# A spectral filter whose column table is stored as even columns, then odd ones, with the weight products on DVE shifted by one channel

## The chip, the cores and the metric

The kernel runs on one core of one Trainium2 chip. The metric is the time of one execution in microseconds (us), as the device counts it; smaller is better. The five engines run their own queues in order and meet through semaphores: TensorE (PE; its weight loads are listed apart as PEld), VectorE (DVE), ScalarE (ACT), GpSimd (POOL) and SyncE (SP), which issues most of the DMA transfers.

## The reference

The input `x` has 2048 rows and 576 columns in bfloat16. The first half is a layer norm, a two-dimensional real FFT, a product with a complex weight per frequency, the inverse FFT, and the addition of `x`. The second half is a layer norm and a gated feed-forward network with 4608 hidden columns, added to its own input.

```python
def _A_ref(x, w_r, w_i):
    B, S, D = x.shape
    X = rfft2(x.astype(jnp.float32), axes=(-2, -1))
    W = w_r + 1j * w_i
    X = X * W
    y = irfft2(X, s=(S, D), axes=(-2, -1)).astype(jnp.bfloat16)
    return y

def _B_ref(x, w_gate, w_up, w_down):
    return (_gelu(x @ w_gate) * (x @ w_up)) @ w_down

h = x + _A_ref(_layernorm(x), w_r, w_i)
h2 = h + _B_ref(_layernorm(h), w_gate, w_up, w_down)
```

## The kernel before

All transforms are matrix products with tables of sines and cosines that the kernel builds itself. The work goes through four stages.

1. **Norm and first row step.** `x` is loaded, normalised row block by row block on DVE, and multiplied on PE by a small table (`row16`, lines 248 to 273). ACT writes the outcome to `Bt`. Beside that, DVE, POOL and ACT build the tables: `DT` and `D3` (columns, lines 307 to 309), from which POOL later fills `DF` (lines 360 and 361) and DVE fills `DI` (line 394, in `late_tables`).
2. **The channel loop** (lines 576 to 602). Eight channels go through it in the order 1, 2, ..., 7, 0. For each channel, `f2` multiplies a part of `Bt` by the column table (12 matmuls of 290 columns, line 439), separately for even and odd output columns, and ACT writes the two halves interleaved into `pq`. `f3` combines them with twiddle factors (8 matmuls of 289 columns, lines 454 and 455), and ACT writes `g` and `hs`. DVE then forms sum and difference (`xab`, lines 481 and 482), two products with the weights (`m`, line 499, twice the size), `za` and `zb` (lines 505 and 506) and two outputs `Zt` (lines 508 and 509): eight DVE instructions for a channel, each pair reading what the pair before wrote. `i3` is the first inverse step: 12 matmuls of 256 columns (lines 533 and 534) with parts of `Zt` as weights, whose results ACT writes to `EO`.
3. **Inverse columns and the addition to `h`.** `inv_cols` (line 559) multiplies `EO` by the column table, ACT scales the outcome into `cs`, `add_rows` (line 635) forms output rows, the second half of them by reading `cs` backwards, and `add_h` (line 646) adds them to `h_sb`. Then follow the second norm's statistics, `norm2` and `flip`, a transposing DMA that puts the normalised rows into `Bt` as `hl`. The groups from the sixth on are added during stage 4.
4. **The feed-forward network** (lines 728 to 780): four row blocks, each with 36 blocks of gate and up products (line 741) and then the down products (line 761).

The order of the instructions on each engine is the order in which the program writes them (`manual_schedule`). In round `i` of the channel loop PE gets, one behind the other: `f2` of channel i, the first half of `f3` of channel i-1, the first third of `i3` of channel i-3, the second half of `f3`, the second third of `i3`, the rest of `f2`, the last third of `i3`. DVE gets all eight instructions of channel i-1 in round i. So the first `i3` of a channel stands on PE two rounds behind the DVE work that it needs. Tiles in PSUM have four buffers, `Zts` has three, `xab`, `g` and `hs` two each.

The lines that say this:

```python
        if 1 <= i <= n:
            f3(order[i - 1], 0)
        if i >= 3 and not last:
            i3(order[i - 3], 0)
        if 1 <= i <= n:
            f3(order[i - 1], 1)
            wmul(order[i - 1], i)
```

Of the kernel before, what the change touches and what calls it, by code (L numbers as in the profile page):

```python
# [9 lines left out]
ACT = mybir.ActivationFunctionType  # L10
# [14 lines left out]
DH = D // 2  # L25
J = D // 2 + 1
JP = J + 1
F = 4608
NFT = F // P
NR = D // 64  # L30
# [9 lines left out]
def kernel_body(  # L40
# [62 lines left out]
    G16 = keep.tile([P, 2, 2, P], BF16, name="G16")  # L103


    DT = keep.tile([P, 2, 2, JP], BF16, name="DT")
    DF = keep.tile([P, 2, JP], BF16, name="DF")
    DI = keep.tile([P, 2, J], BF16, name="DI")
    mv = keep.tile([P, H, 2], FP32, name="mv")
    rstd = keep.tile([P, H], FP32, name="rstd")  # L110
    mv2 = keep.tile([P, H, 2], FP32, name="mv2")
# [72 lines left out]
    iD = tmp("iD", [P, 3], FP32)  # L184
    iota(iD[:], [[P, 3]], 0, 1)
    iJ = tmp("iJ", [P, JP], FP32)
    iota(iJ[:], [[1, JP]])
    make_identity(nc, ident[:])
    rev = tmp("rev", [P, 1])
    iota(rev[:], [[0, 1]], 2 * P - 1, -2)  # L190
# [107 lines left out]
            normalise(V, xn[:, h, :], mv, rstd, h)  # L298
            row16(h)

    D3 = tmp("D3", [P, 2, JP], BF16)
    pr, ab = tmp("pr", [P, 9, P]), tmp("ab", [P, 9, P], FP32)
    wm = [tmp(n, [P, 8 * J], BF16) for n in ("wm_r", "wm_i")]
    xn_pool = tc.tile_pool(name="xn", bufs=1, side="right")
    xn = xn_pool.__enter__().tile([P, H, D], BF16, name="xn")

    def col_sin(r, src, bias):
        A.activation(DT[:, 0:2, r, :], src[:, 0:2], ACT.Sin, bias=bias[:], scale=-2.0 * PI / D)
        A.activation(D3[:, r, :], src[:, 2], ACT.Sin, bias=bias[:], scale=-2.0 * PI / D)

    for h in range(1, 12, 2):
        ln_act(h)
# [44 lines left out]
    evict4(4)  # L357
    evict(8)
    norms(12, 14)
    G.tensor_copy(DF[0:32, :, :], D3[0:32, :, :])  # L360
    G.tensor_copy(DF[96:128, :, :], D3[96:128, :, :])
    evict(10)
    evict4(8)
    norms(14, 16)
# [26 lines left out]
            V.tensor_scalar(w[:, :, 0 : J : J - 1], w[:, :, 0 : J : J - 1], 0.5, None, op0=ALU.mult)  # L391

    def late_tables():
        V.tensor_copy(DI[0 : J - 2 * P, :, :], D3[0 : J - 2 * P, :, 0:J])
        pt = two("pt")
        for x in range(2):
            for p0 in (0, 64):
                T.matmul(
                    pt[p0 : p0 + 64, 0, x * P : (x + 1) * P],
                    lhsT=F16[:, 0, 64 * x : 64 * x + 64],  # L400
                    rhs=ident[:],
                    start=True,
                    stop=True,
                )
        for sign in range(2):
            A.activation(
                G16[:, sign, :, :].rearrange("p x q -> p (x q)"),
                pt[:, 0, 0 : 2 * P],
                ACT.Copy,
                scale=G_SCALE if sign == 0 else -G_SCALE,  # L410
            )
# [10 lines left out]
    NS, C, SN = 0, 1, 2  # L422
    pq = {}
    xab = {}
    zt = {}
    order = [1, 2, 3, 4, 5, 6, 7, 0]

# [4 lines left out]
    def f2(c):  # L432
        ps = two("pq_ps")
        if c == 1:
            fill(ps[:, 0, :], 4)
        col = slice(slot[c] * P, (slot[c] + 1) * P)
        for par in range(2):
            for t in (par, par + 2, 4):
                T.matmul(  # L439
                    ps[:, par, 0:JP],  # L440
                    lhsT=Bt[:, t, col],
                    rhs=DT[:, t // 2, :, par:JP:2] if t < 4 else DF[:, :, par:JP:2],
                    start=(t == par),
                    stop=(t == 4),
                )
        sb = wk.tile([P, 2, JP], BF16, name="pq", tag="pq", bufs=6)
        (V.tensor_copy if c == 9 else A.copy)(
            sb[:].rearrange("p r (j a) -> p r j a", a=2),
            ps[:, :, 0:JP].rearrange("p a (r j) -> p r j a", r=2),
        )  # L450
        pq[c] = sb
# [5 lines left out]
    def f3(k, half):  # L457
        ps = two("gh_ps")
        if k == 0:
            p0, p8 = pq[0], pq[8]  # L460
            t0, t1 = (NS, C) if half else (C, SN)
            for b, kk, p in ((0, 0, p0), (1, 8, p8)):
                comb(ps[:, b, 0:J], kk, t0, p[:, 0, 0:J], t1, p[:, 1, 0:J])
            if half == 0:
                xab[k] = wk.tile([P, 2, 2, JP], BF16, name="xab", tag="xab", bufs=2)
            A.copy(xab[k][:, half, :, 0:J], ps[:, :, 0:J])
            return
        p, q = pq[k], pq[k + 8]
        gh = wk.tile([P, 2, JP], BF16, name="hs" if half else "g", tag="hs" if half else "g", bufs=2)
        for r in range(2):  # L470
            if half:
                comb(ps[:, 1 - r, 0:J], k, C, q[:, r, 0:J], NS, p[:, r, 0:J])
            else:
                comb(ps[:, r, 0:J], k, C, p[:, r, 0:J], SN, q[:, r, 0:J])
        A.copy(gh[:, :, 0:J], ps[:, :, 0:J])
        if half == 0:
            xab[k] = gh
            return
        g, hs = xab[k], gh
        x = xab[k] = wk.tile([P, 2, 2, JP], BF16, name="xab", tag="xab", bufs=2)  # L480
        V.tensor_tensor(x[:, 0, :, 0:J], g[:, :, 0:J], hs[:, :, 0:J], ALU.subtract)  # L481
        V.tensor_tensor(x[:, 1, ::-1, 0:J], g[:, :, 0:J], hs[:, :, 0:J], ALU.add)  # L482

    def wmul(k, i):
        x = xab[k]
        z = Zts[i % 3]
        zt[k] = z
        zv = z[:, 0 : 4 * JP].rearrange("p (a b j) -> p a b j", a=2, b=2)
        sl = slice(k, 18 - k, 17 - 2 * k) if k else slice(0, 9, 8)
        m1, m2 = (wk.tile([P, 2, 2, JP], BF16, name=n, tag=n, bufs=1) for n in ("m1", "m2"))  # L490
        if k:
            za, zb = (wk.tile([P, 2, JP], BF16, name=n, tag=n, bufs=1) for n in ("za", "zb"))
        else:
            za, zb = zv[:, 0], zv[:, 1]

        for j0, j1 in ((0, J),) if k else ((0, P), (P, J)):
            js = slice(j0, j1)
            for w, m in ((WR, m1), (WI, m2)):
                V.tensor_tensor(  # L499
                    m[:, :, :, js],  # L500
                    x[:, :, :, js],
                    w[:, sl, js].unsqueeze(1).to_broadcast([P, 2, 2, j1 - j0]),
                    ALU.mult,
                )
            V.tensor_tensor(za[:, :, js], m1[:, 0, :, js], m2[:, 1, :, js], ALU.subtract)  # L505
            V.tensor_tensor(zb[:, :, js], m1[:, 1, :, js], m2[:, 0, :, js], ALU.add)  # L506
            if k:
                V.tensor_tensor(zv[:, 0, :, js], za[:, :, js], zb[:, ::-1, js], ALU.add)  # L508
                V.tensor_tensor(zv[:, 1, :, js], zb[:, ::-1, js], za[:, :, js], ALU.subtract)  # L509
# [44 lines left out]
    def inv_cols(x, g):  # L554

        ps = two("cs_ps")
        for e in range(2):
            for jt in range(NJT):
                T.matmul(  # L559
                    ps[:, e, 0:J],  # L560
                    lhsT=EO[x][:, e, jt, 2 * g : 2 * g + 2].rearrange("p h e k l -> p (h e k l)"),
                    rhs=DT[:, jt, e, 0:J] if jt < 2 else DI[:, e, :],
                    start=(jt == 0),
                    stop=(jt == NJT - 1),
                )
        t = eop.tile([P, 2, JP], BF16, name="cs", tag="cs", bufs=H)
        if x == 0 or g:
            A.activation(t[:, :, 0:J], ps[:, :, 0:J], ACT.Copy, scale=Y_SCALE)
        else:
            A.activation(t[:, 0, 0:J], ps[:, 0, 0:J], ACT.Copy, scale=Y_SCALE)  # L570
            V.tensor_scalar(t[:, 1, 0:J], ps[:, 1, 0:J], Y_SCALE, None, op0=ALU.mult)
        cs[x, g] = t


# [1 line left out]
    for i in range(n + 1):  # L576
        last = i >= n
        if not last:
            f2(order[i])
        if i == 0:  # L580
            twiddles()
# [3 lines that stand above are left out]
            i3(order[i - 3], 0)  # L585
        if 1 <= i <= n:
            f3(order[i - 1], 1)
            wmul(order[i - 1], i)
        if i >= 3 and not last:
            i3(order[i - 3], 1)  # L590
        if not last:
            f2(order[i] + 8)
        if i == 0:
            weights()
        if i >= 3:
            for jt in range(0 if last else 2, NJT):
                i3(order[i - 3], jt)
        if i == 1:
            late_tables()
            scr_pool.__exit__(None, None, None)  # L600
            eop = ctx.enter_context(tc.tile_pool(name="eop", bufs=1, side="right"))
            EO = [eop.tile([P, 2, NJT, H, 2, 4, 8], BF16, name=f"EO{x}") for x in range(2)]
# [23 lines left out]
    def add_rows(g):  # L626


        ys = [two("y_ps") for _ in range(2)]
        for b, sl in ((0, slice(0, DH)), (1, slice(DH, 0, -1))):  # L630
            for x in range(2):
                for t in range(2):
                    for i in range(2):
                        rows = slice(64 * i, 64 * i + 64)
                        T.matmul(  # L635
                            ys[i][:, b, 0:DH],
                            lhsT=G16[rows, b * t, x, :],
                            rhs=cs[x, g][rows, t, sl],
                            start=(x == t == 0),
                            stop=(x == t == 1),  # L640
                        )
        return ys

    def add_h(h, ys):
        hv = h_sb[:, h, :].rearrange("p (b n) -> p b n", b=2)
        V.tensor_tensor(hv, hv, ys[h % 2][:, :, 0:DH], ALU.add)  # L646

    def add_both(g):
        ys = add_rows(g)
# [177 lines left out]
```

## Time and profile before

| What | Value |
|---|---|
| Time, median of 3 runs | 516.52 us (516.24 to 517.73) |
| Time of the profiled execution | 516.51 us |
| Its span from first to last instruction | 514.7 us |
| PE busy | 499.4 us (97%) |
| DVE busy | 207.4 us (40%) |
| ACT busy | 153.5 us (30%) |
| Channel loop, from the first sum on DVE to its last output | 35.5 to 63.8 us |
| First gate product | 85.45 us |

The profile's page shows the engines' shares, the granted clock (0.9 or more in all 40 slices) and the chain of work that ended last. A timeline lists instructions by start, duration, engine, line and tile; what stands in brackets is idle time before the instruction and what ended it. Weight loads (PEld) run beside matmuls, and matmuls overlap each other, so the distance between two starts says more than the duration.

### The profile page before, as it was taken

To read this page: it belongs to the slowest core of one execution; us is meant where nothing else is said; L and a number is where in the kernel's file an instruction comes from. 1 tells how busy PE (TensorE), PEld (TensorE's weight loads), DVE (VectorE), ACT (ScalarE), POOL (GpSimd) and SP (SyncE) were. 2 spreads that over 40 slices of the span, in tenths; PEclk is the share of its full clock that TensorE was granted. 3 is DMA by queue.
4 is the path that set the end of the run, shared out by engine and by line. 5 is a ranking of instruction groups with operands and counts; after the bars stand their busy time and mean duration, and the time that the engine had idled before them with its cause. 6 is when DMAs were issued, how large, how long until landed. Compare 5 with 4: busy or idle time off the path is not lost.

```text
span 514.7 us, 9918 instructions
## 1 busy us (share of the span) xinstructions
PE 499.4 (97%) x4369; PEld 295.3 (57%) x4369; DVE 207.4 (40%) x381; ACT 153.5 (30%) x262; POOL 34.7 (7%) x94
## 2 busy tenths in 40 slices
PE   6989998999999999999999999999999999999996
PEld 2457765555556774444467754444577544444774
DVE  8979957566551103533321034433301133333000
ACT  7789974232221002332310013233200133323000
POOL 8700011111110000000000000000000000000000
PEclk9999999999999999999999999999999999999999
DMA  8964049799773008997840069987600487780000
GB/s 277 256 126 137 1 139 221 145 175 198 140 140 67 1 1 184 196 191 159 159 83 0 1 141 185 209 157 156 122 1 0 107 156 162 155 159 3 13 13 24
DMA packets 88459, 61.25 MB, mean 119 GB/s; under 512 B 24288, under 2 KB 87136, under 8 KB 88416
## 3 DMA queue, kind: packets, MB, share of 16 engines
q1 hardware_dynamic: 88128, 59.44, 56.7%
q0 software_dynamic: 288, 1.18, 0.7%
q8 instruction: 34, 0.56, 0.5%
q14 instruction: 9, 0.07, 0.1%
HBM read 52.65 MB, written 2.36 MB: 107 GB/s over the span
## 4 chain that ended last, share of the span: by engine, by line
PE 87%; DVE 9%; ACT 1%; POOL 1%; DMA 1%; issue 1%; DVEq 0%; POOLq 0%; ACTq 0%
PE gu L741 54%; PE acc L761 28%; DVE m L499 2%; PE f2t L258 2%; PE y_ps L635 1%; PE cs_ps L559 1%; PE f2t L246 1%; DMA Bt<-hrow 1%; DVE za L505 1%; DVE Zt L508 1%; PE f L267 1%; DVE xab L481 1%; DVE zb L506 1%; DVE xab L482 1%; DVE Zt L509 1%
## 5 line engine op out<-in xcount | busy, mean ns | idle before, releaser
L741 PE MATMUL gu<-Bt,wgu 64*128 64x512 bf16 x2592 | 281.0, 376 | 0.7 <-DMA Bt<-hrow 0.7
L741 PEld LDWEIGHTS <-wgu 64*128 64x128 bf16 x2592 | 131.2, 94 | 148.4 <-issue 1.7
L749 ACT ACTIVATE g_sb<-gu 128x512 f32<-128x512 f32 x144 | 86.0, 597 | 306.0 <-PE gu L741 306.0
L750 DVE TENSOR_TENSOR P_sb<-g_sb,gu 128x512 bf16<-128x512 f32 x144 | 98.7, 685 | 162.3 <-ACT g_sb L749 162.3
L761 PEld LDWEIGHTS <-P_sb 128*128 128x128 bf16 x1152 | 112.4, 98 | 30.6 <-issue 2.4
L761 PE MATMUL acc<-wd_b,P_sb 128*128 128x288 bf16 x768 | 99.3, 286 | 0.0
L773 DVE TENSOR_TENSOR h_sb<-h_sb,acc 128x576 bf16<-128x576 bf16 x15 | 11.3, 754 | 119.1 <-PE acc L761 119.1
L761 PE MATMUL acc<-wd_a,P_sb 128*128 128x288 bf16 x384 | 52.3, 286 | 0.5 <-DVE h_sb L769 0.5
L246 PE MATMUL f2t<-h_sb,ident 128*128 128x512 bf16 x41 | 12.4, 425 | 4.4 <-DMA h_sb<-in_A_x_dram 4.4
L660 DVE TENSOR_SCALAR hrow<-h_sb,mv,rstd 128x1152 bf16<-128x1152 bf16 x16 | 13.8, 865 | 1.9 <-POOL rstd L135 1.9
L135 POOL TENSOR_TENSOR rstd<-rstd,mhalf 128x1 f32<-128x1 f32 (+2 forms) x21 | 14.0, 666 | 1.8
L559 PE MATMUL cs_ps<-DT,EO 128*128 128x289 bf16 x64 | 12.4, 287 | 0.6 <-DVE h_sb L646 0.4
L439 PE MATMUL pq_ps<-DT,Bt 128*128 128x290 bf16 x64 | 12.9, 292 | 0.0
L134 POOL TENSOR_SCALAR rstd<-mv 128x1 f32<-128x1 f32 (+2 forms) x21 | 4.8, 229 | 114.1 <-DVE mv L119 113.3
L646 DVE TENSOR_TENSOR h_sb<-h_sb,y_ps 128x576 bf16<-128x576 bf16 x16 | 11.3, 745 | 2.1 <-PE y_ps L635 2.1
L533 PE MATMUL eo_ps<-TI,Zt 128*128 128x256 bf16 x48 | 11.7, 273 | 0.0
L534 PE MATMUL eo_ps<-TI,Zt 128*128 128x256 bf16 x48 | 11.5, 274 | 0.2
L124 ACT ACTIVATE junk<-h_sb 128x576 bf16<-128x576 bf16 x16 | 10.7, 671 | 2.5 <-DMA h_sb<-in_A_x_dram 2.0
L559 PEld LDWEIGHTS <-EO 128*128 128x128 bf16 x96 | 9.0, 97 | 4.3 <-issue 1.3
L246 PEld LDWEIGHTS <-ident 128*128 128x128 bf16 x45 | 4.7, 105 | 11.3 <-issue 4.9
L258 PE MATMUL f2t<-F,xn 128*128 128x256 bf16 x64 | 9.7, 274 | 1.6 <-DVE xn L138 1.6
L439 PEld LDWEIGHTS <-Bt 128*128 128x128 bf16 x96 | 9.2, 97 | 3.0
(113 smaller groups left out, 247.0 us busy)
## 6 DMA issues: line engine op xcount, KB each, us to landing
wgu<-in_B_w_gate_dram SPq DMA_DIRECT2D x48, 432.0 KB, 5.1
wgu<-in_B_w_up_dram SPq DMA_DIRECT2D x48, 432.0 KB, 6.6
wd_b<-in_B_w_down_dram SPq DMA_DIRECT2D x2, 1728.0 KB, 8.3
h_sb<-in_A_x_dram SPq DMA_DIRECT2D x3, 576.0 KB, 7.3
wd_a<-in_B_w_down_dram SPq DMA_DIRECT2D x1, 1728.0 KB, 9.1
out_dram<-h_sb SPq DMA_DIRECT2D x3, 576.0 KB, 3.3
WR<-in_A_w_r_dram SPq DMA_DIRECT2D x1, 650.2 KB, 10.0
WI<-in_A_w_i_dram SPq DMA_DIRECT2D x1, 650.2 KB, 15.9
```

What stands on the lines that cost most here:

```text
L135: G.tensor_tensor(dst[:, sl], dst[:, sl], mhalf[:, sl], ALU.pow)
L246: T.matmul(dst, lhsT=ident[:], rhs=h_sb[:, 2, 0:512], start=True, stop=True)
L258: T.matmul(f2t[:, h % 2, t * 2 * P : (t + 1) * 2 * P], lhsT=x[:, d0 : d0 + P], rhs=F16[:, n : n + 2, :], start=(n == 0), stop=(n == 1),)
L439: T.matmul(ps[:, par, 0:JP], lhsT=Bt[:, t, col], rhs=DT[:, t // 2, :, par:JP:2] if t < 4 else DF[:, :, par:JP:2], start=(t == par), stop=( ...
L533: T.matmul(ps[:, b], lhsT=zl(*z0), rhs=TI[:, kk_, 1:3, :], start=True, stop=False)
L534: T.matmul(ps[:, b], lhsT=zl(*z1), rhs=TI[:, kk_, 0:2, :], start=False, stop=True)
L559: T.matmul(ps[:, e, 0:J], lhsT=EO[x][:, e, jt, 2 * g : 2 * g + 2].rearrange("p h e k l -> p (h e k l)"), rhs=DT[:, jt, e, 0:J] if jt < 2 e ...
L660: V.tensor_scalar(hrow[:], h_sb[:, h, :].rearrange("p (r k) -> p r k", k=64).unsqueeze(2).to_broadcast([P, NR, 2, 64]), mv2[:, h, 0:1], rs ...
L741: T.matmul(gu[:, c, :], lhsT=w[rows, r, i * P : (i + 1) * P], rhs=hl[tcnk % 2][rows, r, :], start=(r == 0), stop=(r == NR - 1),)
L749: A.activation(g_sb[:], gu[:, 0, :], ACT.Gelu_apprx_tanh)
L750: V.tensor_tensor(P_sb[:, fa + i, :], g_sb[:], gu[:, 1, :], ALU.mult)
L761: T.matmul(acc[:, c, 0:DH], lhsT=P_sb[:, f, st * P : (st + 1) * P], rhs=wd_a[:, f, cc] if f < NWA else wd_b[:, f - NWA, cc], start=(f == 0 ...
```

## The change

Two things are changed.

The column tables `DT`, `DF`, `DI` (and `D3`, from which the last two are filled) hold the even columns first and then the odd ones, 145 of each, with the cosine or sine part as an inner index. `f2` reads 290 elements that lie next to each other, where it read every second element. `inv_cols` reads two runs of 145 elements, where it read one run of 289, and makes one more column. Its results `cs` stay in the even-then-odd order. `add_rows` reads `cs` in two runs of 144, and so `y_ps` holds the even columns and then the odd ones; `add_h` puts them back in place by reading and writing `h_sb` with a step of two elements.

In the channel loop, DVE's sums (now `sums_of`) and the rest (`wmul`) are written in other rounds. Round i gives DVE the two products and `za`, `zb` of channel i-2, then the two sums of channel i-1, then the two `Zt` of channel i-2. The first channel's sums stand alone in round 1, and the last channel (0), whose `xab` ACT writes, gets its DVE work at the end of the last round. The order on PE and ACT stays.

```diff
-    DT = keep.tile([P, 2, 2, JP], BF16, name="DT")
-    DF = keep.tile([P, 2, JP], BF16, name="DF")
-    DI = keep.tile([P, 2, J], BF16, name="DI")
+    DT = keep.tile([P, 2, 2, 2, JH], BF16, name="DT")
+    DF = keep.tile([P, 2, 2, JH], BF16, name="DF")
+    DI = keep.tile([P, 2, 2, JH], BF16, name="DI")
...
-    iota(iJ[:], [[1, JP]])
+    iota(iJ[:], [[1, 2], [2, JH]])
...
     def col_sin(r, src, bias):
-        A.activation(DT[:, 0:2, r, :], src[:, 0:2], ACT.Sin, bias=bias[:], scale=-2.0 * PI / D)
-        A.activation(D3[:, r, :], src[:, 2], ACT.Sin, bias=bias[:], scale=-2.0 * PI / D)
+        s = src[:].rearrange("p t (a j) -> p t a j", a=2)
+        A.activation(DT[:, :, :, r, :], s[:, 0:2], ACT.Sin, bias=bias[:], scale=-2.0 * PI / D)
+        A.activation(D3[:, :, r, :], s[:, 2], ACT.Sin, bias=bias[:], scale=-2.0 * PI / D)
...
-        V.tensor_copy(DI[0 : J - 2 * P, :, :], D3[0 : J - 2 * P, :, 0:J])
+        V.tensor_copy(DI[0 : J - 2 * P], D3[0 : J - 2 * P])
...
-                    rhs=DT[:, t // 2, :, par:JP:2] if t < 4 else DF[:, :, par:JP:2],
+                    rhs=DT[:, t // 2, par] if t < 4 else DF[:, par],
...
-        g, hs = xab[k], gh
+        hk[k] = gh
+
+    def sums_of(k):
+        g, hs = gk[k], hk[k]
         x = xab[k] = wk.tile([P, 2, 2, JP], BF16, name="xab", tag="xab", bufs=2)
         V.tensor_tensor(x[:, 0, :, 0:J], g[:, :, 0:J], hs[:, :, 0:J], ALU.subtract)
         V.tensor_tensor(x[:, 1, ::-1, 0:J], g[:, :, 0:J], hs[:, :, 0:J], ALU.add)
 
-    def wmul(k, i):
+    def wmul(k, i, nxt=None):
...
             V.tensor_tensor(zb[:, :, js], m1[:, 1, :, js], m2[:, 0, :, js], ALU.add)
+            if nxt:
+                sums_of(nxt)
             if k:
                 V.tensor_tensor(zv[:, 0, :, js], za[:, :, js], zb[:, ::-1, js], ALU.add)
...
-                    ps[:, e, 0:J],
+                    ps[:, e, 0:JP],
                     lhsT=EO[x][:, e, jt, 2 * g : 2 * g + 2].rearrange("p h e k l -> p (h e k l)"),
-                    rhs=DT[:, jt, e, 0:J] if jt < 2 else DI[:, e, :],
+                    rhs=DT[:, jt, :, e, :] if jt < 2 else DI[:, :, e, :],
...
             f3(order[i - 1], 1)
-            wmul(order[i - 1], i)
+            if i == 1:
+                sums_of(order[0])
+            else:
+                wmul(order[i - 2], i - 1, order[i - 1])
...
+        if last:
+            wmul(order[i - 1], i)
...
-        for b, sl in ((0, slice(0, DH)), (1, slice(DH, 0, -1))):
+        for b in range(2):
             for x in range(2):
+                if b == 0:
+                    cv = cs[x, g][:].rearrange("p t (q a) -> p t q a", q=2)[:, :, :, 0 : JH - 1]
+                else:
+                    cv = cs[x, g][:, :, 1:J].rearrange("p t (q a) -> p t q a", q=2)[:, :, :, ::-1]
...
-                            rhs=cs[x, g][rows, t, sl],
+                            rhs=cv[rows, t],
...
-        hv = h_sb[:, h, :].rearrange("p (b n) -> p b n", b=2)
-        V.tensor_tensor(hv, hv, ys[h % 2][:, :, 0:DH], ALU.add)
+        hv = h_sb[:, h, :].rearrange("p (b a q) -> p b q a", b=2, q=2)
+        V.tensor_tensor(hv, hv, ys[h % 2][:, :, 0:DH].rearrange("p b (q a) -> p b q a", q=2), ALU.add)
```

More of the change, by code (lines that the diff above doesn't have):

```diff
@@ L27 @@
 JP = J + 1
+JH = JP // 2
 F = 4608
@@ L299, in norms @@
             row16(h)
-    D3 = tmp("D3", [P, 2, JP], BF16)
+    D3 = tmp("D3", [P, 2, 2, JH], BF16)
     pr, ab = tmp("pr", [P, 9, P]), tmp("ab", [P, 9, P], FP32)
@@ L359, in kernel_body @@
     norms(12, 14)
-    G.tensor_copy(DF[0:32, :, :], D3[0:32, :, :])
-    G.tensor_copy(DF[96:128, :, :], D3[96:128, :, :])
+    G.tensor_copy(DF[0:32], D3[0:32])
+    G.tensor_copy(DF[96:128], D3[96:128])
     evict(10)
@@ L424, in kernel_body @@
     xab = {}
+    gk, hk = {}, {}
     zt = {}
@@ L476, in f3 @@
         if half == 0:
-            xab[k] = gh
+            gk[k] = gh
             return
-        g, hs = xab[k], gh
+        hk[k] = gh
+    def sums_of(k):
+        g, hs = gk[k], hk[k]
         x = xab[k] = wk.tile([P, 2, 2, JP], BF16, name="xab", tag="xab", bufs=2)
@@ L567, in inv_cols @@
         if x == 0 or g:
-            A.activation(t[:, :, 0:J], ps[:, :, 0:J], ACT.Copy, scale=Y_SCALE)
+            A.activation(t[:], ps[:, :, 0:JP], ACT.Copy, scale=Y_SCALE)
         else:
-            A.activation(t[:, 0, 0:J], ps[:, 0, 0:J], ACT.Copy, scale=Y_SCALE)
-            V.tensor_scalar(t[:, 1, 0:J], ps[:, 1, 0:J], Y_SCALE, None, op0=ALU.mult)
+            A.activation(t[:, 0, :], ps[:, 0, 0:JP], ACT.Copy, scale=Y_SCALE)
+            V.tensor_scalar(t[:, 1, :], ps[:, 1, 0:JP], Y_SCALE, None, op0=ALU.mult)
         cs[x, g] = t
```

## The prediction

> **What bounds the kernel now.** I read the page first, for the chain that ended last, then busy time by stage, the chain in order of time around the end of the channel loop, and the timelines of DVE, PE and ACT inside the loop.
>
> ```profile
> span 514.7 us, 9918 instructions
> ...
> PE 87%; DVE 9%; ACT 1%; POOL 1%; DMA 1%; issue 1%; DVEq 0%; POOLq 0%; ACTq 0%
> ```
>
> PE holds 87% of the chain, nearly all in the feed-forward stage, which the change doesn't touch. DVE's 9% is where the change can act. The next row is the stretch of the channel loop: length, then busy time of PE, PEld, DVE, ACT and POOL.
>
> ```profile
> 29.80:63.90 34.10, 33.17 (x260) 24.29 (x260) 30.36 (x65) 30.87 (x50) 0.00 (x0) 1.00 0.29 80
> ```
>
> Three engines are nearly full here. Whichever is relieved, another stands close behind, so the question is not how much DVE saves but where PE stands then. The chain, in order of time (start, length, what):
>
> ```profile
> 63.39 0.38 DVE Zt L509
> ...
> 63.81 0.28 PE eo_ps L534
> 64.10 0.11 PE eo_ps L533
> ...
> 71.95 1.41 DVE h_sb L646 x2
> ...
> 76.66 0.66 DVE h_sb L646
> ...
> 81.89 3.42 DMA Bt<-hrow
> ...
> 85.45 4.69 PE gu L741 x41
> ```
>
> Up to 63.8 us DVE's last `Zt` sets the end; from there PE, then three additions to `h_sb` with norm work between, the last flip, and the gate products. What is won before 63.8 us is handed down to the end if the later links keep their length.
>
> The DVE timeline: the loop's first sum, the `DI` copy, one full channel, and the loop's last output.
>
> ```profile
> 35.48 0.47 DVE L481 TENSOR_TENSOR xab<-g,hs 128x578 bf16<-128x578 bf16 x1 [0.69 <-ACT hs L475]
> ...
> 39.44 0.30 DVE L394 COPY DI<-D 33x578 bf16<-33x578 bf16 x1
> 39.66 0.45 DVE L481 TENSOR_TENSOR xab<-g,hs 128x578 bf16<-128x578 bf16 x1
> ...
> 51.59 0.46 DVE L481 TENSOR_TENSOR xab<-g,hs 128x578 bf16<-128x578 bf16 x1
> 51.96 0.46 DVE L482 TENSOR_TENSOR xab<-g,hs 128x578 bf16<-128x578 bf16 x1
> 52.45 0.77 DVE L499 TENSOR_TENSOR m<-xab,WR 128x1156 bf16<-128x1156 bf16 x1
> 53.13 0.76 DVE L499 TENSOR_TENSOR m<-xab,WI 128x1156 bf16<-128x1156 bf16 x1
> 53.93 0.47 DVE L505 TENSOR_TENSOR za<-m,m 128x578 bf16<-128x578 bf16 x1
> 54.31 0.46 DVE L506 TENSOR_TENSOR zb<-m,m 128x578 bf16<-128x578 bf16 x1
> 54.87 0.47 DVE L508 TENSOR_TENSOR Zt<-za,zb 128x578 bf16<-128x578 bf16 x1
> 55.25 0.46 DVE L509 TENSOR_TENSOR Zt<-zb,za 128x578 bf16<-128x578 bf16 x1
> 55.62 0.46 DVE L481 TENSOR_TENSOR xab<-g,hs 128x578 bf16<-128x578 bf16 x1
> ...
> 63.30 0.46 DVE L509 TENSOR_TENSOR Zt<-zb,za 128x578 bf16<-128x578 bf16 x1
> ```
>
> DVE never idles: 4.03 us from sum to sum (51.59 to 55.62). An instruction that doesn't read the one right before it starts 0.37 us after a 578-element one, before that one has ended (51.59 to 51.96; 55.25 to 55.62). One that does read it waits for its end: 0.49 (51.96 to 52.45), 0.80 against 0.68 (53.13 to 53.93), 0.56 (54.31 to 54.87).
>
> PE in the same stretch: starts of the first `i3` matmuls of each round, six `f2` matmuls, and the inverse columns behind the loop.
>
> ```profile
> 39.60 0.27 PE L534 MATMUL eo_ps<-TI,Zt 128*128 128x256 bf16 x1
> ...
> 43.75 0.28 PE L534 MATMUL eo_ps<-TI,Zt 128*128 128x256 bf16 x1
> ...
> 47.71 0.28 PE L534 MATMUL eo_ps<-TI,Zt 128*128 128x256 bf16 x1
> ...
> 48.98 0.42 PE L439 MATMUL pq_ps<-DT,Bt 128*128 128x290 bf16 x2
> ...
> 49.76 0.27 PE L533 MATMUL eo_ps<-TI,Zt 128*128 128x256 bf16 x1
> ...
> 51.46 0.27 PE L533 MATMUL eo_ps<-TI,Zt 128*128 128x256 bf16 x1
> 51.74 0.28 PE L534 MATMUL eo_ps<-TI,Zt 128*128 128x256 bf16 x1
> ...
> 55.76 0.28 PE L534 MATMUL eo_ps<-TI,Zt 128*128 128x256 bf16 x1
> ...
> 61.05 0.41 PE L559 MATMUL cs_ps<-DT,EO 128*128 128x289 bf16 x2
> ...
> 62.91 0.41 PE L559 MATMUL cs_ps<-DT,EO 128*128 128x289 bf16 x2
> ...
> 63.16 0.28 PE L559 MATMUL cs_ps<-DI,EO 128*128 128x289 bf16 x1
> ...
> 63.94 0.27 PE L533 MATMUL eo_ps<-TI,Zt 128*128 128x256 bf16 x1
> ```
>
> In each round PE stops at the second `i3` matmul until `Zt` is there. Without that stop a round would take 51.46 + 0.11 - 47.71 = **3.86 us** (0.11 is the regular distance in the chain's rows). The four rounds from 39.60 to 55.76 took 16.16; four times 3.86 is 15.44, so PE lost 0.72 there. At the end, the row of 63.94 would stand at 63.16 + 0.12 + 0.11 + 0.11 = 63.50: 0.44 more. **PE loses 1.16 us** to DVE in all. DVE may save more than that, and it won't show.
>
> **The change part by part, against the profiled execution (516.51 us, 0.01 under the median of the runs, 1.8 over its span).**
>
> *DVE's order.* The eight instructions stay, but three pairs now have others between them. A round's distances become: product to product 0.68, product to `za` 0.80 (still dependent), 0.38, `zb` to sum 0.37, 0.37, sum to `Zt` 0.37, 0.38, `Zt` to next product 0.37: **3.72 us** instead of 4.03. So DVE becomes faster than PE's 3.86.
>
> *Where `Zt` comes later.* The first channel's `Zt` now stands behind the second channel's sums and the `DI` copy. The first sum starts at 35.44 (six faster `f2` matmuls ahead of it, below); then 35.81, the copy at 36.18, products at 36.40 (0.22 behind the copy, as 39.44 to 39.66) and 37.08, `za` 37.88, `zb` 38.26, sums 38.63 and 39.00, `Zt` 39.37 and 39.75, done at 40.21. PE's second `i3` matmul starts 0.05 after that (63.30 + 0.46 to 63.81), at 40.26, where it was 39.60. **A new wait of 0.66 us.** Behind it PE's queue holds the second half of `f3`, and behind that ACT's `hs` and DVE's next sums.
>
> *Does PE wait again?* `Zt` of round n is done at 40.21 + 3.72n, PE arrives at 40.26 + 3.79n: no. The sums need `hs`, and these two rows of ACT give its place:
>
> ```profile
> 52.82 0.65 ACT L475 CAST hs<-gh_ps 128x578 bf16<-128x578 f32 x1 [0.34 <-PE gh_ps L455]
> ...
> 56.85 0.64 ACT L475 CAST hs<-gh_ps 128x578 bf16<-128x578 f32 x1 [0.34 <-PE gh_ps L455]
> ```
>
> `hs` ends 1.73 after the second `i3` matmul (51.74 to 53.47). In the fifth round that is 40.26 + 15.16 + 1.73 = 57.15; DVE comes to those sums at 38.63 + 18.60 = 57.23, so there is just no wait. ACT is busy 4.03 - 0.34 = 3.69 of a round and fits into 3.79. The last `Zt` of channel 7 (dependent again, no sums between) is done near 62.0, and PE gets to it at 63.0: DVE, late by up to a microsecond, would still be covered.
>
> *`f2` read without gaps.* Six matmuls take 49.76 - 48.98 = 0.78, so 0.130 each; inverse columns, read in one run, take (62.91 - 61.05) / 15 = 0.124. The only difference in what PE reads as the moving operand is the step of two. I take 0.124 for `f2` after: 12 x 0.006 = 0.07 a round, 3.79 instead of 3.86, **0.28** over the four rounds PE is the bound. The lower bound is 0; a gain past 0.28 is excluded by 290 columns against 289.
>
> [...]
>
> *Inverse columns in two runs, one more column.* 48 matmuls stand between the loop and the first addition: 8 calls of six. One column is 0.0004 us each (0.124 / 289): 0.02 in all. For two runs there is no row, since every moving operand here is one run; nearest is one run itself (0) and the stepped one (+0.006, 0.29 in all). I take 0, since one break in 290 elements is nearer to none than to 290 steps. A gain is excluded. The same for `add_rows`, 8 pairs before the first addition: 0 to 0.05.
>
> *Addition with a step of two* (groups up to 150 us: count, busy, mean ns, idle before).
>
> ```profile
> L750 DVE TENSOR_TENSOR P_sb<-g_sb,gu 128x512 bf16<-128x512 f32 x31 | 21.0, 679 | 26.8 <-ACT g_sb L749 26.8
> ...
> L646 DVE TENSOR_TENSOR h_sb<-h_sb,y_ps 128x576 bf16<-128x576 bf16 x16 | 11.3, 745 | 2.1 <-PE y_ps L635 2.1
> ...
> L547 DVE CAST EO<-eo_ps 128x512 bf16<-128x512 f32 x1 | 0.7, 691 | 1.2 <-PE eo_ps L534 1.2
> ```
>
> [...] `EO`, written in scattered runs of eight, costs 691 ns, as `P_sb` in one run does at 679. I take 0. The upper end, half the rate, is +0.60 each; three are on the chain (two at 71.95, one at 76.66), the fourth falls into a wait for POOL.
>
> *At nothing:* the tables' `Sin`, copies and `iota` have the same sizes; the last channel's DVE work moves behind `i3` in the text but stays last on DVE, before 63.0. No DMA moves on SP or POOL; the flips and the loads of stage 4 follow the chain.
>
> **Sum:** 1.16 of waits gone, 0.66 of new wait, 0.28 from `f2`, 0.02 for the column: 1.16 - 0.66 + 0.28 - 0.02 = 0.76. 516.51 - 0.76 = 515.75, so **515.7 us**, 0.15% faster, less than the 0.3% (1.55 us) that I count as told from no change.
>
> **Rivals.**
>
> - *`f2` gains nothing* (the 0.006 has another cause): 516.0.
> - *Two runs cost what a step costs* on inverse columns and rows: +0.34, 516.1.
> - *The new DVE order saves no time.* Were every DVE instruction to start only when the one before has ended its flush, DVE would stay at 4.03 and the last `Zt` where it is: 516.5. The 0.37 against 0.49 in the rows speaks against it. [...]
> - *Slower: the stepped addition.* It decides from 0.76 / 3 = 0.25 us more for one addition. At the upper end, 3 x 0.60 = 1.80 on the way to the last flip: 516.51 - 0.76 + 1.80 = 517.55, and about 518 if the following six additions also hold back the PSUM buffers of the first gate product. For it: no row has a step of one element on DVE. [...]
> - *More than 0.3% faster.* All that the loop holds is 1.16 + 0.28 + 0.04, 1.48 us; it would take a gain that no row shows, 514.9 or less.
>
> **How the numbers follow.** Chances: my forecast 0.56 (its own range 515.4 to 516.0), `f2` nothing 0.08, two runs 0.09, no saving on DVE 0.05, slower 0.12, faster than the loop holds 0.10. The forecast and the three rivals beside it all lie within 0.3%: 0.78. The range, 515.0 to 517.0, takes these in, with the beginnings of the outer two.
>
> **What would show it.** On DVE: sums between `zb` and `Zt`, 3.7 to 3.8 us a round, with gaps ahead of the sums. On PE: one wait of about 0.66 at the first `i3`, near 40.26, none in the rounds behind and none before channel 7; `f2` distances of 0.124, inverse columns unchanged. The addition's mean near 745 ns. The first gate product near 84.7. I am wrong if PE still waits for `Zt` in each round, if ACT's `hs` runs late and drags DVE, or if the additions are longer.

## The result, and the profile after

The changed kernel takes 515.74 us in the median of 18 runs (515.4 to 517.11); the kernel before, run beside it, takes 516.48. The ratio is 0.9985, with a 95% interval of 0.9978 to 0.9992: a small gain that is real, 0.74 us in the medians, where 0.76 was forecast. A few runs of either kernel are some 1.3 us longer, and the ratio and its interval count them.

From the page of the changed kernel, the chain that ended last by engine:

```profile
PE 91%; DVE 5%; ACT 1%; POOL 1%; DMA 1%; issue 1%; POOLq 0%; DVEq 0%; ACTq 0%
```

DVE's share of the chain fell from 9% to 5%, PE's rose from 87% to 91%: the loop's bound changed hands. How is seen in the timeline of DVE (start, length, line, tile): the copy of `DI`, the end of the first channel, one full round, and channel 7's last output.

```profile
36.21 0.30 DVE L396 COPY DI<-D 33x580 bf16<-33x580 bf16 x1
...
39.75 0.46 DVE L517 TENSOR_TENSOR Zt<-zb,za 128x578 bf16<-128x578 bf16 x1
...
51.22 0.76 DVE L505 TENSOR_TENSOR m<-xab,WR 128x1156 bf16<-128x1156 bf16 x1
51.89 0.76 DVE L505 TENSOR_TENSOR m<-xab,WI 128x1156 bf16<-128x1156 bf16 x1
52.68 0.47 DVE L511 TENSOR_TENSOR za<-m,m 128x578 bf16<-128x578 bf16 x1
53.06 0.46 DVE L512 TENSOR_TENSOR zb<-m,m 128x578 bf16<-128x578 bf16 x1
53.43 0.46 DVE L487 TENSOR_TENSOR xab<-g,hs 128x578 bf16<-128x578 bf16 x1
53.80 0.46 DVE L488 TENSOR_TENSOR xab<-g,hs 128x578 bf16<-128x578 bf16 x1
54.17 0.46 DVE L516 TENSOR_TENSOR Zt<-za,zb 128x578 bf16<-128x578 bf16 x1
54.54 0.46 DVE L517 TENSOR_TENSOR Zt<-zb,za 128x578 bf16<-128x578 bf16 x1
54.91 0.76 DVE L505 TENSOR_TENSOR m<-xab,WR 128x1156 bf16<-128x1156 bf16 x1
...
61.41 0.46 DVE L517 TENSOR_TENSOR Zt<-zb,za 128x578 bf16<-128x578 bf16 x1
```

A round is 3.69 us (51.22 to 54.91), where it was 4.03. The only distance that still waits for the instruction ahead is the one to `za`, 0.79 (0.67 from product to product). The sum now follows `zb` after 0.37 and `Zt` follows the sum after 0.37.

PE, from the timeline: the first `i3` matmuls, the one wait left behind them, and the third `i3` matmul of channel 7, which stood at 63.94 before.

```profile
39.89 0.28 PE L541 MATMUL eo_ps<-TI,Zt 128*128 128x256 bf16 x1 [0.39 <-DVE Zt L516]
40.26 0.28 PE L542 MATMUL eo_ps<-TI,Zt 128*128 128x256 bf16 x1
...
58.62 0.28 PE L457 MATMUL gh_ps<-pq,TF 128*128 128x289 bf16 x1 [0.38 <-ACT pq L450]
...
63.13 0.27 PE L541 MATMUL eo_ps<-TI,Zt 128*128 128x256 bf16 x1
```

And the chain of waits in order of time, which now runs on PE through the whole loop:

```profile
40.26 0.28 PE eo_ps L542
...
41.69 0.74 PE pq_ps L442 x6
...
71.17 1.47 DVE h_sb L663 x2
...
73.63 0.48 issue
...
81.15 3.38 DMA Bt<-hrow
...
84.67 5.34 PE gu L758 x47
```

Six `f2` matmuls take 0.74 instead of 0.78. The loop hands over 0.81 us earlier (63.94 to 63.13), the first gate product begins 0.78 earlier (85.45 to 84.67), and the span is shorter by about as much (514.7 to 514.0). Below, "the gate" is the start of the first gate product: what is won or lost ahead of it carries over to the end.

### The profile page after: what moved, and what is told of

It is laid out like the page before. It is cut to its first block, busy times and chain, and to the rows that moved or that the text cites. A ratio compares the mean times of both kernels' runs of the same rounds, so it can differ in the third digit from the quotient of the medians.

```text
span 514.0 us, 9918 instructions
## 1 busy us (share of the span) xinstructions
PE 498.3 (97%) x4369; PEld 295.3 (57%) x4369; DVE 206.5 (40%) x381; ACT 153.5 (30%) x262; POOL 34.6 (7%) x94
## 4 chain that ended last, share of the span: by engine, by line
PE 91%; DVE 5%; ACT 1%; POOL 1%; DMA 1%; issue 1%; POOLq 0%; DVEq 0%; ACTq 0%
PE gu L758 55%; PE acc L778 28%; PE f2t L259 2%; PE pq_ps L442 1%; PE cs_ps L567 1%; PE eo_ps L542 1%; PE eo_ps L541 1%; PE y_ps L652 1%; PE f2t L247 1%; DMA Bt<-hrow 1%; PE gh_ps L457 1%; PE gh_ps L458 1%; PE f L268 1%; DVE st L119 0%; DVE h_sb L663 0%
## 5 line engine op out<-in xcount | busy, mean ns | idle before, releaser
L567 PE MATMUL cs_ps<-DT,EO 128*128 128x290 bf16 x64 | 12.5, 286 | 0.6 <-DVE h_sb L663 0.4
L652 PE MATMUL y_ps<-cs,G 64*128 64x288 bf16 x128 | 9.8, 283 | 1.1 <-DVE h_sb L663 0.9
```

The lines of the kernel that those rows point to most:

```text
L567: T.matmul(ps[:, e, 0:JP], lhsT=EO[x][:, e, jt, 2 * g : 2 * g + 2].rearrange("p h e k l -> p (h e k l)"), rhs=DT[:, jt, :, e, :] if jt < 2 ...
L652: T.matmul(ys[i][:, b, 0:DH], lhsT=G16[rows, b * t, x, :], rhs=cv[rows, t], start=(x == t == 0), stop=(x == t == 1),)
```

## Experiments

**The tables alone.** DVE keeps its old order of eight instructions for one channel.

```diff
-            if i == 1:
-                sums_of(order[0])
-            else:
-                wmul(order[i - 2], i - 1, order[i - 1])
+            if order[i - 1]:
+                sums_of(order[i - 1])
+            wmul(order[i - 1], i)
...
-        if last:
-            wmul(order[i - 1], i)
```

> The new column tables with DVE's old order. My theory (DVE's dependent chain sets the end of the loop, so a faster f2 only makes PE wait longer): DVE rounds stay at 4.03 us, first gate product at 85.4 (before: 85.45), time 516.4 to 516.5. Rival (the two parts add up, f2's 0.28 us counts by itself): first gate product near 85.2, time 516.2.

Measured: 516.56 us, ratio to the kernel before 0.9999 (0.9990 to 1.0007). The timelines of DVE and of PE:

```profile
51.58 0.46 DVE L487 TENSOR_TENSOR xab<-g,hs 128x578 bf16<-128x578 bf16 x1
...
55.60 0.46 DVE L487 TENSOR_TENSOR xab<-g,hs 128x578 bf16<-128x578 bf16 x1
```

```profile
85.46 1.90 PE L755 MATMUL gu<-Bt,wgu 64*128 64x512 bf16 x16 [0.62 <-DMA Bt<-hrow]
```

A DVE round is 4.02 us and the gate stays where it was. The faster `f2` is worth nothing while PE waits for DVE anyway.

**DVE's order alone.** The old tables, the stepped reads of `f2`, the addition in one run.

```diff
-    DT = keep.tile([P, 2, 2, 2, JH], BF16, name="DT")
+    DT = keep.tile([P, 2, 2, JP], BF16, name="DT")
...
-                    rhs=DT[:, t // 2, par] if t < 4 else DF[:, par],
+                    rhs=DT[:, t // 2, :, par:JP:2] if t < 4 else DF[:, :, par:JP:2],
```

> DVE's new order with the old column tables and the old addition. My theory: DVE rounds of 3.70 us, PE bound at 3.86 us a round after one wait of 0.7 us; 1.16 - 0.70 = 0.46 us gained, first gate product near 85.0, time 516.05. Rival (DVE's order alone brings all of it and f2 nothing): first gate product at 84.7, time 515.75.

Measured: 515.99 us, ratio 0.9990 (0.9981 to 0.9999). PE's timeline:

```profile
48.02 0.27 PE L541 MATMUL eo_ps<-TI,Zt 128*128 128x256 bf16 x1
...
51.87 0.27 PE L541 MATMUL eo_ps<-TI,Zt 128*128 128x256 bf16 x1
...
84.94 2.33 PE L753 MATMUL gu<-Bt,wgu 64*128 64x512 bf16 x20 [0.71 <-DMA Bt<-hrow]
```

PE's round is 3.85 us without a wait, as computed from the kernel before (3.86), and the gate comes 0.51 us earlier. So the tables alone bring 0.0, DVE's order alone 0.5, both together 0.78: `f2`'s gain counts only once PE is the bound.

**Is the first channel on the path, and the last not?** Two more copies of `DI`'s size in front of the first channel's products, then three in front of channel 7's, each kernel executed once.

```diff
+        if k == 1:
+            for _ in range(2):
+                V.tensor_copy(spare[0 : J - 2 * P], DI[0 : J - 2 * P])
```

> The changed kernel with two more copies of DI's size (0.22 us each, into a spare tile) on DVE ahead of the first channel's products. My theory: all later PE work 0.44 us later, first gate product at 85.1. Rival (DVE's first channel has slack): 84.67.

> The changed kernel with three more copies (0.66 us) ahead of channel 7's products once more, because in the first execution TensorE's clock was at half for a while ahead of the loop and everything stood 1.25 us later. My theory: first gate product at 84.67, as in the changed kernel. Rival (DVE's last Zt still sets the end of the loop): 85.3.

Measured: 516.47 us with the gate at 85.39 for the first, 515.74 us with the gate at 84.68 for the last. Of the run with the copies ahead of the first channel, the copies on DVE and the second `i3` matmul on PE (40.26 in the changed kernel):

```profile
36.55 0.64 DVE L505 COPY spare<-DI 33x580 bf16<-33x580 bf16 x2
```

```profile
40.95 0.28 PE L546 MATMUL eo_ps<-TI,Zt 128*128 128x256 bf16 x1
```

Of the run with the later copies, DVE's timeline and PE's:

```profile
58.64 0.98 DVE L505 COPY spare<-DI 33x580 bf16<-33x580 bf16 x3
...
62.31 0.46 DVE L521 TENSOR_TENSOR Zt<-zb,za 128x578 bf16<-128x578 bf16 x1
```

```profile
62.92 0.27 PE L545 MATMUL eo_ps<-TI,Zt 128*128 128x256 bf16 x1
```

Channel 7's `Zt` is done at 62.77 instead of 61.87 and PE still finds it ready. Ahead of the first channel the two copies cost 0.68 on DVE (each started 0.34 after the copy before it, which it depends on, and not 0.22), PE's first wait grew by 0.69, and the gate moved by 0.72. So DVE's first channel sets the end, one for one, and its last doesn't.

An earlier execution of the second kernel took 517.04 us, with the gate at 85.97: its granted clock was 0.996 in the mean (1.000 in the other), the four matmuls ahead of the first `f2` and the eighteen of `f2` behind them took 1.56 and 3.36 us where the changed kernel's took 1.02 and 2.22, and it stood 1.25 us later from there on (first `f3` matmul at 34.79, 33.54 in the changed kernel). PE found channel 7's `Zt` ready there too (done at 64.01, PE at 64.16). Its expectation:

> The changed kernel with three more such copies (0.66 us) on DVE ahead of channel 7's products. My theory (PE comes to channel 7 about 1.1 us after its Zt): nothing moves, first gate product at 84.67. Rival (DVE's last Zt still sets the end of the loop, as in the kernel before): 85.3.

**More work in front of the first wait.** The first third of `i3` goes behind the second half of `f3` on PE, in every round.

```diff
             f3(order[i - 1], 0)
-        if i >= 3 and not last:
-            i3(order[i - 3], 0)
-        if 1 <= i <= n:
             f3(order[i - 1], 1)
...
         if i >= 3 and not last:
+            i3(order[i - 3], 0)
             i3(order[i - 3], 1)
```

> The changed kernel with the first third of i3 written behind the second half of f3 on PE, so that 0.49 us of matmuls stand ahead of the first wait. My theory: the wait at the first i3 (0.81 us against an unhindered start) shrinks to 0.32, all later PE work moves 0.49 earlier, first gate product at 84.2, time 515.25. Rival (the wait only moves, because ACT or DVE closes the loop at the old place): first gate product between 84.5 and 84.7, time 515.6 or more.

Measured: 515.08 us, ratio 0.9969 (0.9959 to 0.9979), PE's timeline:

```profile
40.27 0.28 PE L542 MATMUL eo_ps<-TI,Zt 128*128 128x256 bf16 x1
...
57.97 0.28 PE L457 MATMUL gh_ps<-pq,TF 128*128 128x289 bf16 x1 [0.22 <-ACT pq L450]
...
84.06 3.20 PE L756 MATMUL gu<-Bt,wgu 64*128 64x512 bf16 x28 [0.66 <-DMA Bt<-hrow]
```

`Zt` comes at the same time, but four more matmuls are done by then. The gate is 0.61 earlier, 0.12 more than the 0.49 of the matmuls. The rest comes from PE's wait for ACT's `pq` in the last round, which is 0.22 here and 0.38 in the changed kernel.

**The `DI` copy on POOL.**

```diff
-        V.tensor_copy(DI[0 : J - 2 * P], D3[0 : J - 2 * P])
+        G.tensor_copy(DI[0 : J - 2 * P], D3[0 : J - 2 * P])
```

> The changed kernel with the copy of DI moved from DVE to POOL. My theory (from the first i3 on PE never stops for DVE, so the first Zt sets everything behind it): the first Zt comes 0.22 us earlier, PE's first wait shrinks by 0.22, first gate product at 84.45 (changed kernel: 84.67), time 515.5. Rival (another engine, ACT's hs or the last DVE work, is the real bound by then): 84.67 and 515.74, unchanged.

Measured: 515.34 us, ratio 0.9984 (0.9973 to 0.9995), the gate at 84.26: 0.41 earlier. But the second `i3` matmul stands at 40.18, only 0.08 earlier. I had counted the copy at its distance of 0.22. In the kernel before, the first product, right behind the sum that it reads, starts 0.49 after it (35.86 to 36.35); in the changed kernel, with the copy between them, 0.59 after it (35.84 to 36.43). The copy mostly stood in that wait, so moving it frees little. The rest arises after the loop, in POOL's timeline, here of the changed kernel and then of this one:

```profile
74.11 0.23 POOL L135 TENSOR_SCALAR rstd<-mv 128x1 f32<-128x1 f32 x1 [47.48 <-DVE mv L120]
```

```profile
73.67 0.23 POOL L135 TENSOR_SCALAR rstd<-mv 128x1 f32<-128x1 f32 x1 [46.31 <-DVE mv L120]
```

In the changed kernel the chain has 0.48 of "issue" ahead of this instruction; here it begins 0.44 earlier though its input came only 0.08 earlier. Counted from its semaphore, POOL begins after 0.50 in the changed kernel (0.02 in its queue and the 0.48) and after 0.13 here (0.02 and 0.11). To tell apart whether that hangs on the copy's being gone from DVE or on one more instruction in POOL's queue, the next kernel leaves the copy on DVE and adds a memset to POOL:

```diff
         V.tensor_copy(DI[0 : J - 2 * P], D3[0 : J - 2 * P])
+        G.memset(DI[96:128], 0.0)
```

> The changed kernel with one more instruction in POOL's queue (a memset of rows of DI that are zero already, right after the table work; the copy of DI stays on DVE). It asks where the 0.41 us of the run with the copy on POOL came from, of which only 0.08 arose in the channel loop; in that run POOL's first instruction after the loop began 0.13 us after its semaphore, against 0.50 in the changed kernel. Theory A (the 0.50 hangs on the instruction's place in POOL's code, so one more instruction anywhere ahead moves it): 0.13 here too, first gate product at 84.3, time 515.4. Theory B (it hangs on the copy being gone from DVE): 0.50, 84.67, 515.74.

Measured: 515.28 us, ratio 0.9971 (0.9962 to 0.9981), with POOL, the chain's row ahead of POOL's, and PE as follows:

```profile
73.76 0.23 POOL L135 TENSOR_SCALAR rstd<-mv 128x1 f32<-128x1 f32 x1 [46.60 <-DVE mv L120]
```

```profile
73.65 0.11 issue
```

```profile
84.36 2.98 PE L759 MATMUL gu<-Bt,wgu 64*128 64x512 bf16 x26 [0.68 <-DMA Bt<-hrow]
```

An added instruction that computes nothing new brings the gate 0.31 us forward (84.67 to 84.36) and the median 0.46. So the copy's being gone from DVE isn't needed, and theory B falls. The length of the wait is no reason either: the kernel with the later `i3` waits 46.84 us on POOL and has 0.49 of issue, this one waits 46.60 and has 0.11. All three kernels with one more instruction on POOL have 0.11, all the others 0.48 or 0.49. But the copy and the memset stand at the same place in POOL's queue, so "anywhere ahead" isn't shown, and the cause of the delay stays open.

**Both together**, the copy on POOL and the later `i3`.

> The changed kernel with the copy of DI on POOL and the first third of i3 behind the second half of f3. My theory: both shorten the same wait, 0.49 and 0.22 of its 0.81 us, so 0.71 together: first gate product at 83.95, time 515.05, faster than both kernels. Rival (only one of the two counts): 84.2, time 515.25.

Measured: 514.64 us, ratio 0.9963 (0.9950 to 0.9975), the gate at 83.59: faster than both kernels. It beats its forecast by 0.4. POOL's earlier start (0.37) was in no term of it; the other two misses, 0.12 too little for the later `i3` and 0.14 too much for the copy, nearly cancel.

**What a step costs PE.** `f2` reads its moving operand from `Bt` in sixteen shapes; the product with the column table is left out (one execution).

```diff
+    reads = [Bf[:, 0:N2], Bf[:, 0:N2], Bf[:, 1 : N2 + 1]]
+    reads += [Bf[:, 0 : 2 * N2 : 2], Bf[:, 1 : 2 * N2 : 2]]
+    reads += [Bf[:, 0 : s * N2 : s] for s in (3, 4, 8, 16, 32)]
...
     def f2(c):
+        rhs = reads.pop(0)
...
-                    rhs=DT[:, t // 2, par] if t < 4 else DF[:, par],
+                    rhs=rhs,
```

> The changed kernel with f2's moving operand taken from Bt in sixteen shapes, one for each call of f2 (the product with the column table is left out, so the output is not the reference's): step 1 (from an even and an odd element), 2 (even, odd), 3, 4, 8, 16, 32; two runs of 145, 29 runs of 10, 145 runs of 2; backwards with step 1 and 2. My theory: distances of 0.124 us for one run, 0.130 for step 2 from either start, 0.124 for two runs, and more than 0.130 for the larger steps. [...]

In PE's timeline a row of six matmuls is six distances long and 0.16 to 0.18 for the tail of the last. In order: step 2 from an even and an odd element; step 3 alone, then 3 and 4; 8; 16; 32; two runs of 145; 29 runs of 10; 145 runs of 2; backwards by 1 and by 2; step 1.

```profile
36.09 0.94 PE L453 MATMUL pq_ps<-Bt 128*128 128x290 bf16 x6
37.20 0.95 PE L453 MATMUL pq_ps<-Bt 128*128 128x290 bf16 x6
38.97 1.33 PE L453 MATMUL pq_ps<-Bt 128*128 128x290 bf16 x6
...
38.97 2.88 PE L453 MATMUL pq_ps<-Bt 128*128 128x290 bf16 x12
43.55 3.23 PE L453 MATMUL pq_ps<-Bt 128*128 128x290 bf16 x6
47.23 3.31 PE L453 MATMUL pq_ps<-Bt 128*128 128x290 bf16 x6
53.83 3.08 PE L453 MATMUL pq_ps<-Bt 128*128 128x290 bf16 x6
57.28 1.66 PE L453 MATMUL pq_ps<-Bt 128*128 128x290 bf16 x6
61.46 0.91 PE L453 MATMUL pq_ps<-Bt 128*128 128x290 bf16 x6
62.64 1.71 PE L453 MATMUL pq_ps<-Bt 128*128 128x290 bf16 x6
66.04 0.91 PE L453 MATMUL pq_ps<-Bt 128*128 128x290 bf16 x6
67.23 0.95 PE L453 MATMUL pq_ps<-Bt 128*128 128x290 bf16 x6
69.87 0.90 PE L453 MATMUL pq_ps<-Bt 128*128 128x290 bf16 x6
```

The clock was not whole throughout: the table of stretches (after each window: its length, the busy time of PE, its weight load, DVE, ACT and POOL, then the granted clock, the DMA share and GB/s) shows two of them at half, 0.50:

```profile
47.20:51.00 3.80, 3.80 (x11) 1.21 (x9) 0.63 (x2) 1.20 (x3) 0.00 (x0) 0.50 0.00 0
...
57.30:60.00 2.70, 2.70 (x13) 1.71 (x12) 0.59 (x2) 1.47 (x4) 0.00 (x0) 0.50 0.00 0
```

| Read | Row, us | One matmul, us |
|---|---|---|
| step 1 | 0.90 | 0.123 |
| step 1 backwards; 29 runs of 10 | 0.91 | 0.125 |
| step 2, even or odd start, backwards | 0.94, 0.95, 0.95 | 0.130 to 0.132 |
| step 3 | 1.33 | 0.195 |
| step 4 | 2.88 less six of 0.195 | 0.258 |
| 145 runs of 2, one in 8 elements | 1.71 | 0.258 |
| step 8 | 3.23 | 0.51 |
| step 16 (half clock), 32 | 3.31, 3.08 | 0.52, 0.48 |
| two runs of 145 (half clock) | 1.66 | 0.25 |

Both of my statements hold: the 0.006 of `f2` comes from the step, whichever element it starts from, and two runs are free: 29 runs of 10 take 0.125 at whole clock, and the two runs of 145 met half clock, where `f3`'s matmuls of 289 columns in one run stand 0.24 apart as well (58.97 to 59.21). Step 4 takes 0.258, twice the 0.123 of step 1.

## Why the prediction was right

- **What bounds.** That DVE's saving counts only up to what PE waits for it is borne out: DVE's last `Zt` came 1.9 us earlier (63.30 to 61.41), but PE's work behind it only 0.81. The two parts of the sum were also measured one by one: 1.16 - 0.66 = 0.50 was forecast for DVE's order, and alone it brought the gate 0.51 forward; 0.26 was forecast for the tables, and they brought 0.27 more.
- **DVE's order.** 3.72 us a round was forecast, 3.69 came. One sign named for DVE, gaps ahead of the sums, didn't show: the sum follows `zb` after 0.37, and after 0.38 in the last round (56.76 to 57.14). That agrees with the prediction's own working, by which `hs` comes just in time (57.15 against 57.23; it ended at 57.10).
- **The new wait.** Forecast: second `i3` matmul at 40.26, 0.66 later than before. It stands at 40.26. That this wait is on the path is shown by the copies ahead of the first channel and by the later `i3`.
- **No wait after it.** PE's rounds run without a stop up to the wait for ACT's `pq` in the last round. The prediction named no such wait and put it at nothing without a reason. The kernel before has it too, and it grew by only 0.04, so the sum holds:

```profile
59.00 0.28 PE L454 MATMUL gh_ps<-pq,TF 128*128 128x289 bf16 x1 [0.34 <-ACT pq L447]
```

  Channel 7's `Zt` was ready at 61.87 for a PE that came at 62.91; the three copies show that the slack is real.
- **`f2`.** 0.124 was forecast from the inverse columns; six in 0.74 are 0.123, and PE's round is 3.78 (44.05 to 47.83) where 3.79 was forecast. That the step is the cause and not something else, as the rival of an `f2` that gains nothing has it, is settled by the shapes: 0.130 to 0.132 with a step of two, 0.123 without.
- **Inverse columns and rows.** No cost was forecast for two runs: none is found (18 inverse column matmuls in 2.24, 60.67 to 62.91, are 0.124 each, as before).
- **The addition.** Zero was forecast; the list of its sixteen instructions before and after (least, median, longest, ns) shows a little:

```profile
L646 DVE TENSOR_TENSOR h_sb<-h_sb,y_ps x16: 702/747/754, 71.9 to 149.7; 128x576 bf16<-128x576 bf16 x16
```

```profile
L663 DVE TENSOR_TENSOR h_sb<-h_sb,y_ps x16: 749/783/800, 71.2 to 149.0; 128x576 bf16<-128x576 bf16 x16
```

  That is 0.036 us each, far from the 0.25 at which the slower rival decides. No run shows that rival's upper end of 0.60 for an addition; it was my estimate, and these 0.036 came in its place. On the chain two take 1.47 instead of 1.41 and the third 0.70 instead of 0.66; with the work between them, 0.74 of the loop's 0.81 is left at the last flip (81.89 to 81.15). The flip took 0.04 less (3.42 to 3.38), which hides half of that; that these small errors cancel is luck.
- **What was sized wrongly** is a step of an experiment, not of the sum: I took the `DI` copy to cost its distance of 0.22, but it filled a gap between two dependent instructions and cost 0.08. POOL's first instruction behind the loop (0.37) and ACT's `pq` (0.16 with the later `i3`) lie outside what the prediction called all that the loop holds, 1.48; with both of them the kernel with both edits brings the gate 1.86 forward (85.45 to 83.59).

The rivals: that DVE's new order saves no time is refuted by the 0.37 between `zb` and the sum, which begins 0.09 before the end of `zb` (0.46), and no run shows a flush that would hold it back; `f2` gaining nothing, by the gate, which comes at 84.94 with DVE's order alone and at 84.67 with the tables too.

## What to carry to other kernels

When three engines are nearly full, work out from the starts in the trace how long the second one waits for the first: that is all that relieving the first can bring (here 1.16 us), and a saving on the second counts only together with it (here 0.27 with it, 0.0 alone). A shift by one step breaks dependent pairs (here 0.37 us between two instructions in place of 0.49 and 0.56), but it delays the first output (here by 0.66); look at what that first delay costs, and put other work in front of it: here that brought nearly as much again as the whole change (0.61 us at the gate, against 0.78).

## What the runs showed of the hardware

- **PE's moving operand.** Step 8 takes 0.51 us for 290 columns, steps 16 and 32 no more (0.52, 0.48), and runs of two elements in every eight take the same 0.258 as step 4. An estimate from these: PE takes the longer of the columns' own 0.123 and 1.76 ns for each stretch of eight bfloat16 elements touched (0.51 / 290; 0.258 / 145 = 1.78). It gives 0.191 for step 3 (0.195 measured), is 6% high for step 32, and gives 72.5 stretches or 0.128 us for step 2, just over 0.123, where 0.130 was measured. Step 16 at half clock (0.52) takes about what step 8 takes at whole clock (0.51), from which I estimate that the price hardly follows TensorE's clock; no run has a step of 8 or more at both clocks.
- **POOL's first instruction after a wait of 46 to 48 us** began 0.13 us after its semaphore when a copy or a memset stood behind the table work in its queue, and 0.50 us after it without.
- **A step of two elements on DVE.** An addition of 576 elements took 0.783 us in the median with it and 0.747 (1.3 ns an element) with the elements next to each other: 0.036 more.
